# A searched order of one core's 2,098 operations, replaced by another searched order

## Chip, core and metric

The kernel runs on one core of a Trainium2 chip, in one launch. The core has five engines with a queue each: TensorE (PE; its weight loads are listed as PEld), VectorE (DVE), ScalarE (ACT), GpSimd (POOL) and SyncE (SP), which issues nearly all transfers here. An engine runs its own queue strictly in order and waits for others through semaphores. The metric is the time of one execution on the device in microseconds; smaller is better. The median of three runs is compared.

## What is computed

A linear-attention layer (a state of 48 x 48 per head, decayed by `w` at each step) over 4 batches, 8 heads and 768 steps, and behind it a feed-forward layer whose gate is a sigmoid of a short convolution:

```python
def _attn_ref(r, k, v, w, u):
    for t in range(S):
        cur = np.einsum('bhd,bhe->bhde', u[None] * kt, vt)
        y[:, :, t] = np.einsum('bhd,bhde->bhe', rt, state + cur)
        state = wt[:, :, :, None] * state + np.einsum('bhd,bhe->bhde', kt, vt)
...
def _moe_ref(x, w_in, conv_w, w_out):
    h = np.maximum(x @ w_in, 0.0)
    for k in range(K):
        conv_out += conv_w[k][None, None, :] * hp[:, k:k + S, :]
    gate = 1.0 / (1.0 + np.exp(-conv_out))
    return (h * gate @ w_out).astype(np.float32)
```

`x` is the attention's output with the heads side by side, 384 wide; `w_in` is 384 x 1024, `w_out` 1024 x 384, the convolution has three taps. `moe_w_in`, `moe_conv_w` and `moe_w_out` come as 64-bit floats and are turned into pairs of 32-bit numbers on the chip.

## The kernel before

The sequence is cut into 24 chunks of 128 steps, six for each batch. One chunk goes through these steps, named by their lines:

- Loads of `w`, `k`, `r`, `v` (L560, on SP). ScalarE rearranges a little of each (L583, operation `fill`). TensorE turns w, k and r (L605 for chunks 0 to 7; from chunk 8 on as half-transposes, L735, in two sets `f1` and `f2` around the scores of the chunk before). VectorE zeroes four columns of the bank that holds w (L575, `pad`), runs two scans over w (L615 and L623, a reciprocal L619 between them) and multiplies them into k and r (L620, L627).
- The rest of each head's rows is brought to a tile `last`: by TensorE (L636, `gather`) for chunks 0 to 3, by six small transfers (L644) for the others. TensorE turns the scaled keys back (L668 or within L735), ScalarE copies them (L677, L678).
- GpSimd multiplies r, k and u (L652, L654), VectorE sums (L655), GpSimd writes the sums on the diagonal of a tile `pm` (L658). TensorE makes the scores (L719), VectorE copies the upper triangle of them into `pm` (L751, twice a chunk).
- The state: TensorE L765, VectorE adds it to the decayed old one (L769, or L771 for a batch's first chunk), with ScalarE and GpSimd preparing the old one (L704, L707, L711). The output of the chunk: TensorE L781 (from the state) and L796 (within the chunk); ScalarE and VectorE write it as a high and a low part into `xT` (L800, L801).

A block of the feed-forward layer is 384 steps, half a batch: eight times a product with `w_in` (L810, three operations of three matmuls each), the gate (ScalarE L822, L823, L828, L831; VectorE L824, L826, L829; GpSimd L832), and then for three groups of 128 rows a product with `w_out` of eight operations (L839), an output copy (L867) and a store (L868). Weights are loaded in pieces of up to 1152 KB (L538, L546), and each 128 x 384 of them is converted by ScalarE (L490, L492), VectorE (L494, L497) and GpSimd (L499), and split (L478, L479). The small convolution weights are loaded by L523 and converted in four VectorE instructions (L463, L467, L469, L471), one of ScalarE (L465, which needs L463) and one of GpSimd (L473).

Nothing is scheduled by the compiler. The program records its 2,098 operations with their dependences (`Plan.op`) and then issues them in the order of a table, `ORDER`. A negative entry is a warm-up matmul of no use to the result (L446) into the bank of that number. Another table, `PLACES`, gives to each tile, in the order in which they are first needed, the slot of its store: 8 PSUM banks, 12 strips of 384 columns, 6 tiles for loaded w, k, r, 6 for weights and so on. So the tables set each engine's queue and which earlier use of a slot a new tile has to wait for.

```python
        for i in ORDER:
            if i < 0:
                self.warm(self.spare[-1 - i])
                continue
            _, _, f, deps, bufs = self.ops[i]
            assert deps <= done
            for b in bufs:
                if b.t is None:
                    b.t = b.view(b.store[next(places)])
            f()
```

Ahead of the table's operations stand a few fixed ones: five junk matmuls (L369), constants and zeroed tiles. Operation 20 broadcasts u with two matmuls (L650).

Of the kernel before, what the change touches and what calls it, by code (L numbers as in the profile page):

```python
# [28 lines left out]
    190, 0, 1, 2, 231, 51, 192, 20, 194, 4, -8, -8, -8, -8, -8, -8, -8, -8, -8, -8, -8, 198, -8, -8, -8, -8, 8, 191,  # L29
    60, 197, 200, 202, 205, 5, 6, 21, -8, -8, -8, -8, 11, -8, -8, -8, -8, 16, 22, 23, 238, 7, 10, 12, 13, 15, 17,  # L30
    52, 55, 24, 235, 53, 239, 210, 25, 56, 241, 243, 54, 246, 195, 196, 9, -4, -4, -4, -4, -4, -4, 18, 19, 199, 206,
    201, 207, 203, 182, 26, 183, -2, 208, 57, 211, 63, 212, 279, 68, 70, 71, 233, 237, 247, 248, 184, 62, 61, 64,
    214, 232, 272, 27, 14, 28, 236, 276, 209, 58, 251, 213, 252, 65, 216, 69, 59, 75, 215, 240, 280, 242, 3, 273,
    274, 278, 277, 431, 222, 185, 282, 284, 244, 224, 77, 186, 78, 253, 223, 287, 255, 72, 218, 292, 293, 249, 193,
    234, 29, 256, 435, 257, 76, 79, 439, 219, 181, 220, 217, 440, 221, 281, 250, 204, 288, 283, 225, 187, 227, 266,
    228, 289, 285, 432, 433, 275, 476, 82, 478, 477, 634, 296, 226, 294, 438, 290, 259, 441, 258, 260, 267, 443,
    446, 32, 188, 80, 262, 73, 254, 74, 286, 229, 81, 300, 295, 230, 30, 436, 297, 31, 291, 301, 455, 33, 437, 298,
    66, 44, 261, 456, 34, 189, 39, 46, -5, -5, 442, 263, 265, 264, 304, 37, 40, 306, 447, 268, 269, 38, 303, 302,
    299, 480, 484, 45, 270, 485, 35, 47, 305, 41, 67, 48, 98, 97, 309, 271, 448, 310, 311, 482, 444, 99, 457, 100,
    483, -3, -3, -3, 459, 83, 101, 500, 36, 312, 307, 486, 488, 491, 85, 86, 492, 92, 308, 493, 357, 358, 359, 346,  # L40
    347, 348, 481, 42, 84, 49, 90, 245, 91, 461, 102, 360, 361, 460, 638, 43, 87, 103, 487, 50, 463, 501, 362, 363,
    93, 94, 104, 349, 350, 489, 121, 107, 351, 352, 674, 453, 451, 747, 449, 434, 450, 454, 452, 120, 119, 364, 105,
# [900 lines left out]
```

## Time and profile before

| what | value |
|---|---|
| median of 3 runs | 335.58 us (334.97 to 335.73) |
| the profiled execution, and its span | 335.81 us, 333.5 us |
| TensorE busy, weight loads busy | 320.4 us (96%), 299.4 us (90%) |
| VectorE, ScalarE, GpSimd busy | 259.0 us (78%), 233.0 us (70%), 182.4 us (55%) |
| bytes moved, mean rate | 39.30 MB, 118 GB/s |
| granted TensorE clock, mean | 0.997 |

Busy time is the union of an engine's records. A matmul's record includes its way through the engine and overlaps the next one's, so that a stretch can be full of matmuls though one could start sooner; a weight load belongs to each matmul, and these do not overlap. The shares are means over the span: VectorE is full in the first third and half empty in the last. The span runs from the first to the last instruction; the rest of the execution's time lies around it.

### The profile page before, as it was taken

How to read it: one execution, taken by the hardware profiler on the slowest of the kernel's cores; microseconds unless marked ns; L12 is line 12 of the kernel's file. 1: busy time of each engine (PE TensorE's matmuls, PEld its weight loads, DVE VectorE, ACT ScalarE, POOL GpSimd, SP SyncE). 2: the span in 40 equal slices, each digit the busy share in tenths (PEclk: the TensorE clock that was granted, in tenths of full speed). 3: DMA queues.
4: the chain of work that ended last, by engine and by line, in shares of the span. 5: the costliest groups of instructions: out<-in, count | busy, mean ns of one | idle time of the engine just before them, and what ended most of it. 6: DMA issues, size and time to landing. Idle time of an engine off the chain costs nothing.

```text
span 333.5 us, 10276 instructions
## 1 busy us (share of the span) xinstructions
PE 320.4 (96%) x3979; PEld 299.4 (90%) x3979; DVE 259.0 (78%) x508; ACT 233.0 (70%) x644; POOL 182.4 (55%) x221
## 2 busy tenths in 40 slices
PE   8789999999999999999999999999999999999994
PEld 5668888898989899998999999999999999999994
DVE  1999999999998889988877988869876885575200
ACT  3369999998895478778776576846766768885411
POOL 7368997988874650378465440295525414533600
PEclk9999999999999999999999999999999999999998
DMA  7988969735254685466226836218400650000005
GB/s 144 242 178 220 247 170 232 248 73 109 42 113 79 138 235 139 107 176 128 56 61 131 234 88 135 63 33 173 108 3 17 200 168 0 2 0 2 0 22 197
DMA packets 113818, 39.30 MB, mean 118 GB/s; under 512 B 102349, under 2 KB 109286, under 8 KB 113766
## 3 DMA queue, kind: packets, MB, share of 16 engines
q1 hardware_dynamic: 113764, 38.61, 47.5%
q8 instruction: 32, 0.52, 0.7%
q14 instruction: 20, 0.16, 0.2%
q10 hardware_dynamic: 2, 0.00, 0.0%
HBM read 31.88 MB, written 4.72 MB: 110 GB/s over the span
## 4 chain that ended last, share of the span: by engine, by line
PE 49%; DMA 2%; DVE 1%; ACT 1%; issue 0%; SPq 0%; ACTq 0%
PE bank L839 22%; PE bank L810 16%; PE bank L719 3%; PE bank L796 3%; PE bank L735 2%; PE bank L781 2%; DMA nat<-in_w_dram 2%; PE bank L765 1%; DVE strip L824 1%; DVE strip L826 0%; ACT strip L823 0%; DVE strip L829 0%; DVE kr L620 0%; ACT strip L828 0%; ACT strip L867 0%
## 5 line engine op out<-in xcount | busy, mean ns | idle before, releaser
L810 PE MATMUL bank<-xT,wi 128*128 128x386 f32 x576 | 112.3, 343 | 1.3 <-DVE strip L497 0.7
L839 PE MATMUL bank<-wo,gh 128*128 128x384 f32 x576 | 109.2, 339 | 0.2 <-DVE strip L497 0.2
L810 PEld LDWEIGHTS bank<-xT,wi 128*128 128x128 f32 x576 | 100.9, 189 | 4.1 <-DVE strip L497 1.0
L839 PEld LDWEIGHTS bank<-wo,gh 128*128 128x128 f32 x576 | 100.5, 188 | 1.4 <-DVE strip L497 0.5
L832 POOL TENSOR_TENSOR gh<-strip,gh 128x384 fp32r<-128x384 f32 x64 | 64.5, 1025 | 58.9 <-ACT gh L831 48.2
L824 DVE SCALAR_TENSOR_TENSOR strip<-bank,cw,strip 128x384 f32<-128x384 f32 x64 | 38.2, 609 | 13.2 <-ACT strip L823 13.1
L829 DVE TENSOR_TENSOR strip<-bank,strip 128x384 f32<-128x384 f32 x64 | 34.7, 553 | 13.1 <-ACT strip L828 11.0
L828 ACT ACTIVATE strip<-strip 128x384 f32<-128x384 f32 x64 | 32.6, 522 | 14.1 <-DVE strip L826 14.0
L658 POOL TENSOR_SCALAR_AFFINE_SELECT pm<-dg 128x1024 f32<-128x1024 f32 x24 | 27.2, 1133 | 24.9 <-DVE dg L655 18.8
L822 ACT ACTIVATE bank<-bank 128x386 f32<-128x386 f32 x64 | 30.1, 478 | 14.5 <-PE bank L810 14.2
L826 DVE SCALAR_TENSOR_TENSOR strip<-bank,cw,strip 128x384 f32<-128x384 f32 x64 | 38.5, 613 | 1.2
L823 ACT ACTIVATE strip<-bank,cw 128x384 f32<-128x384 f32 x64 | 36.6, 580 | 3.1 <-DMA out_dram<-strip 1.0
L751 DVE COPY_PREDICATED pm<-upper,bank 128x512 f32<-128x512 int32 x48 | 33.9, 735 | 6.2 <-PE bank L719 4.5
L652 POOL TENSOR_TENSOR strip<-nat,nat 128x384 f32<-128x384 f32 x24 | 24.4, 1017 | 23.4 <-PE bank L796 8.6
L831 ACT CAST gh<-strip 128x384 fp32r<-128x384 f32 x64 | 31.6, 510 | 4.0 <-DVE strip L829 3.9
L796 PE MATMUL bank<-pm,strip 128*32 128x128 f32 x384 | 25.2, 273 | 0.0
L796 PE MATMUL bank<-pm,vz 128*32 128x128 f32 x384 | 24.9, 272 | 0.0
L654 POOL TENSOR_TENSOR strip<-strip,ubc 128x384 f32<-128x384 f32 x24 | 24.4, 1019 | 0.6
L867 ACT COPY strip<-bank 128x384 f32<-128x384 f32 x24 | 11.2, 477 | 18.5 <-PE bank L839 18.0
L615 DVE TENSOR_TENSOR_SCAN kr<-bank,one_end 128x387 f32<-128x387 f32 x24 | 22.8, 951 | 1.4 <-DMA last<-kr 0.5
L623 DVE TENSOR_TENSOR_SCAN kr<-bank,dA 128x387 f32<-128x387 f32 x24 | 22.9, 956 | 0.4
L583 ACT COPY nat<-nat 128x96 f32<-128x96 f32 x72 | 18.4, 269 | 7.0 <-DMA nat<-in_w_dram 3.9
(104 smaller groups left out, 518.3 us busy)
## 6 DMA issues: line engine op xcount, KB each, us to landing
gh<-in_moe_w_out_dram SPq DMA_DIRECT2D x5, 1152.0 KB, 6.9
nat<-in_w_dram SPq DMA_DIRECT2D x24, 192.0 KB, 3.6
nat<-in_k_dram SPq DMA_DIRECT2D x24, 192.0 KB, 3.6
nat<-in_r_dram SPq DMA_DIRECT2D x24, 192.0 KB, 3.7
gh<-in_moe_w_in_dram SPq DMA_DIRECT2D x4, 1152.0 KB, 7.3
strip<-in_v_dram SPq DMA_DIRECT2D x24, 192.0 KB, 3.2
out_dram<-strip SPq DMA_DIRECT2D x24, 192.0 KB, 2.1
last<-kr SPq DMA_DIRECT2D x120, 16.2 KB, 2.4
```

What stands on the lines that cost most here:

```text
L751: op("DVE", "cp", lambda g=g: nc.vector.copy_predicated(out=pm.t[:, g], mask=upper.unsqueeze(1).to_broadcast([P, NP, L]), data=sc[g].t.rea ...
L796: nc.tensor.matmul(rows(a, 32), lhsT=lhs, rhs=pm.t[:, g, j, :], start=(c == 0 and i == 0), stop=(i == 3), skip_group_check=True)
L810: nc.tensor.matmul(t.t[:, 0:xs.stop - xs.start], lhsT=wi[:, m, a, f * P:(f + 1) * P], rhs=xT[:, x0 + m, c, xs], start=(m == 0 and j == 0), ...
L822: ("ACT", "relu", lambda: nc.scalar.activation(out=h(0, width + 2), in_=h(0, width + 2), func=AF.Relu), [t], [t]),
L823: ("ACT", "mul", lambda: nc.scalar.mul(out=a(), in_=h(1), mul=cw[:, 1, fs]), [t, "cw"], [a1]),
L824: ("DVE", "stt", lambda: nc.vector.scalar_tensor_tensor(out=a(), in0=h(0), scalar=cw[:, 0, fs], in1=a(), op0=ALU.mult, op1=ALU.add), [t], ...
L826: ("DVE", "stt", lambda: nc.vector.scalar_tensor_tensor(out=a(), in0=h(2), scalar=cw[:, 2, fs], in1=a(), op0=ALU.mult, op1=ALU.add), [t], ...
L828: ("ACT", "sig", lambda: nc.scalar.activation(out=a(), in_=a(), func=AF.Sigmoid), [], [a1]),
L829: ("DVE", "gate", lambda: nc.vector.tensor_tensor(out=g.t[:, 0:width], in0=h(1), in1=a(), op=ALU.mult), [t, a1], [g]),
L831: ("ACT", "cast", lambda: nc.scalar.copy(out=part(0)[:, 0:width], in_=g.t[:, 0:width]), [g], [key]),
L832: ("POOL", "lo", lambda: nc.gpsimd.tensor_tensor(out=part(1)[:, 0:width], in0=g.t[:, 0:width], in1=part(0)[:, 0:width].bitcast(F32), op=AL ...
L839: nc.tensor.matmul(acc.t[:, 0:DM], lhsT=part(a)[:, tt * P:(tt + 1) * P], rhs=wo[:, f, c, :], start=(f == 0 and a + c == 0), stop=(f == FT ...
```

## The change

The tables `ORDER` and `PLACES` are replaced; the rest of the file is the same. The same 2,098 operations are issued in another order, with 29 warm-up matmuls in place of 35. The new order was searched for with some slack added to each hand-over between engines and to each transfer, and with longer steps on all engines but TensorE.

```diff
 ORDER = [
-    190, 0, 1, 2, 231, 51, 192, 20, 194, 4, -8, -8, -8, -8, -8, -8, -8, -8, -8, -8, -8, 198, -8, -8, -8, -8, 8, 191,
...
+    0, 1, 190, 51, 4, 20, -8, 8, 2, 231, 191, 192, 3, 55, 7, 52, 10, 56, 197, 194, 53, 5, 12, 54, 238, -8, -8, -8,
...
```

Three places show what moves. In the rows, a number behind a tile's name tells its slot, so that `kr_139` and `kr_140` are two of three slots for scaled keys, and `strip_119` in L463 to L471 is the loaded convolution weights.

The first is the head of VectorE's queue behind its fixed instructions. Before:

```order
L575 MEMSET bank_65 128x4
L615 SCALAR_TENSOR_TENSOR kr_139<-bank_65,one_end 128x387
L619 RECIPROCAL dA_137<-kr_139 128x3
L623 SCALAR_TENSOR_TENSOR kr_139<-bank_65,dA_137 128x387
L575 MEMSET bank_69 128x4
L575 MEMSET bank_66 128x4
L615 SCALAR_TENSOR_TENSOR kr_140<-bank_66,one_end 128x387
L619 RECIPROCAL dA_137<-kr_140 128x3
L620 TENSOR_TENSOR kr_140<-bank_67,kr_140 128x3x128
L623 SCALAR_TENSOR_TENSOR kr_140<-bank_66,dA_137 128x387
L627 TENSOR_TENSOR kr_140<-bank_68,kr_140 128x3x128
L463 TENSOR_SCALAR bank_70<-strip_119 24x128
```

And now:

```order
L469 TENSOR_SCALAR bank_66<-strip_119 24x128
L575 MEMSET bank_65 128x4
L463 TENSOR_SCALAR bank_67<-strip_119 24x128
L615 SCALAR_TENSOR_TENSOR kr_139<-bank_65,one_end 128x387
L471 SCALAR_TENSOR_TENSOR strip_121<-strip_119,bank_66 24x128
L575 MEMSET bank_66 128x4
L619 RECIPROCAL dA_137<-kr_139 128x3
L467 SCALAR_TENSOR_TENSOR strip_122<-strip_119,bank_67 24x128
L575 MEMSET bank_68 128x4
L623 SCALAR_TENSOR_TENSOR kr_139<-bank_65,dA_137 128x387
L615 SCALAR_TENSOR_TENSOR kr_140<-bank_66,one_end 128x387
L620 TENSOR_TENSOR kr_139<-bank_69,kr_139 128x3x128
```

Two of the four instructions on the convolution weights and one bank's zeroing now stand ahead of the first scan, and the first scans are those of chunk 0, where they were those of chunk 1.

The second is the head of SP's queue, all loads. Before:

```order
L560 DMA nat_131<-in_w_dram 128x8x48
L560 DMA nat_132<-in_w_dram 128x8x48
L560 DMA nat_133<-in_k_dram 128x8x48
L560 DMA nat_134<-in_r_dram 128x8x48
L560 DMA nat_135<-in_w_dram 128x8x48
L523 DMA strip_119<-in_moe_conv_w_dram 24x256
L560 DMA nat_136<-in_r_dram 128x8x48
L560 DMA nat_131<-in_k_dram 128x8x48
L538 DMA gh<-in_moe_w_in_dram 128x3x768
L560 DMA nat_132<-in_r_dram 128x8x48
L560 DMA nat_133<-in_k_dram 128x8x48
L560 DMA nat_134<-in_w_dram 128x8x48
```

And now:

```order
L560 DMA nat_134<-in_r_dram 128x8x48
L560 DMA nat_135<-in_w_dram 128x8x48
L560 DMA nat_136<-in_k_dram 128x8x48
L560 DMA nat_131<-in_r_dram 128x8x48
L560 DMA strip_120<-in_v_dram 128x8x48
L538 DMA gh<-in_moe_w_in_dram 128x3x768
L560 DMA nat_133<-in_r_dram 128x8x48
L560 DMA nat_132<-in_k_dram 128x8x48
L560 DMA nat_134<-in_w_dram 128x8x48
L560 DMA nat_135<-in_r_dram 128x8x48
L538 DMA gh<-in_moe_w_in_dram 128x3x768
L560 DMA strip_128<-in_v_dram 128x8x48
```

The four rows ahead of these, not shown, are the loads of w and k of chunk 0, w of chunk 1 and the convolution weights, which stood sixth. The second piece of `w_in` stands fifteenth now and ahead of a `v` (of chunk 1), where it stood nineteenth and behind three of them.

The third is VectorE's queue around the zeroing of the bank for the transposed w of chunk 12, on which the half-transposes of TensorE behind it wait (the last row of each piece). Before:

```order
L824 SCALAR_TENSOR_TENSOR strip_122<-bank_64,cw,strip_122 128x384
L826 SCALAR_TENSOR_TENSOR strip_122<-bank_64,cw,strip_122 128x384
L751 COPY_PREDICATED pm_159<-upper,bank_65 128x512
L615 SCALAR_TENSOR_TENSOR kr_140<-bank_66,one_end 128x387
L619 RECIPROCAL dA_137<-kr_140 128x3
L623 SCALAR_TENSOR_TENSOR kr_140<-bank_66,dA_137 128x387
L751 COPY_PREDICATED pm_159<-upper,bank_70 128x512
L620 TENSOR_TENSOR kr_140<-bank_69,kr_140 128x3x128
L627 TENSOR_TENSOR kr_140<-bank_71,kr_140 128x3x128
L829 TENSOR_TENSOR strip_119<-bank_64,strip_122 128x384
L575 MEMSET bank_66 128x4
```

And now:

```order
L615 SCALAR_TENSOR_TENSOR kr_140<-bank_68,one_end 128x387
L655 TENSOR_REDUCE dg_157<-strip_129 128x4x2
L769 TENSOR_TENSOR sd_167<-bank_65,sd_166 112x192
L619 RECIPROCAL dA_137<-kr_140 128x3
L623 SCALAR_TENSOR_TENSOR kr_140<-bank_68,dA_137 128x387
L620 TENSOR_TENSOR kr_140<-bank_71,kr_140 128x3x128
L627 TENSOR_TENSOR kr_140<-bank_70,kr_140 128x3x128
L751 COPY_PREDICATED pm_159<-upper,bank_66 128x512
L655 TENSOR_REDUCE dg_158<-strip_119 128x4x2
L751 COPY_PREDICATED pm_159<-upper,bank_69 128x512
L575 MEMSET bank_64 128x4
```

In both orders the same instructions stand ahead of that zeroing, in another sequence, but for the one L769, which stands right behind it in the old order.

## Rows read from the trace of the kernel before

**Rows 1.** Stretches: busy us (instructions) of each engine, granted clock, DMA.
```profile
core 0: us, PE busy (x) PEld busy (x) DVE busy (x) ACT busy (x) POOL busy (x), PEclk, DMA share, GB/s
8.00:20.00 12.00, 9.21 (x79) 7.47 (x77) 11.38 (x26) 4.88 (x18) 6.05 (x7) 1.00 0.91 215
20.00:40.00 20.00, 18.96 (x435) 16.63 (x439) 19.72 (x41) 17.94 (x60) 17.30 (x20) 1.00 0.89 210
40.00:60.00 20.00, 19.10 (x241) 16.81 (x231) 19.38 (x41) 18.90 (x53) 17.62 (x22) 1.00 0.74 200
60.00:80.00 20.00, 19.11 (x145) 17.81 (x137) 18.92 (x37) 18.14 (x46) 16.96 (x18) 1.00 0.52 150
80.00:108.00 28.00, 27.32 (x406) 25.20 (x406) 26.97 (x53) 22.26 (x69) 20.87 (x23) 1.00 0.44 87
```

**Rows 2.** Waits of VectorE: us in total, times, longest.
```profile
DVE bank L575 <- PE bank L605: 5.6, 1, 5.6
```

**Rows 3.** Timeline of VectorE, 7 to 14 us: start, us, instruction, idle before.
```profile
7.61 0.06 DVE L575 MEMSET bank<- 128x4 f32 x1 [5.61 <-PE bank L605]
7.78 0.96 DVE L615 TENSOR_TENSOR_SCAN kr<-bank,one_end 128x387 f32<-128x387 f32 x1
...
13.43 0.27 DVE L463 TENSOR_SCALAR bank<-strip 24x128 int32<-24x128 int32 x1
```

**Rows 4.** Timeline of ScalarE, 3 to 8 us, and of SP, 4 to 6.
```profile
3.64 0.27 ACT L583 COPY nat<-nat 128x96 f32<-128x96 f32 x1 [0.79 <-DMA nat<-in_w_dram]
...
5.57 0.27 ACT L583 COPY nat<-nat 128x96 f32<-128x96 f32 x1 [0.68 <-DMA nat<-in_k_dram]
...
4.75 0.98 SPq L523 DMA_DIRECT2D strip<-in_moe_conv_w_dram  x1
```

**Rows 5.** Timeline of TensorE, 4 to 8.2 us.
```profile
4.47 2.53 PE L446 MATMUL bank<-ident 128*128 128x256 bf16 x11
6.79 0.74 PE L605 MATMUL bank<-ident,nat 128*128 128x128 f32 x3
...
7.80 0.49 PE L605 MATMUL bank<-ident,nat 128*128 128x128 f32 x3
```

**Rows 6.** VectorE by line, 8 to 108 us: busy us, mean ns, idle before.
```profile
L826 DVE SCALAR_TENSOR_TENSOR strip<-bank,cw,strip 128x384 f32<-128x384 f32 x16 | 9.7, 614 | 0.4
L824 DVE SCALAR_TENSOR_TENSOR strip<-bank,cw,strip 128x384 f32<-128x384 f32 x16 | 9.5, 607 | 0.0
...
L829 DVE TENSOR_TENSOR strip<-bank,strip 128x384 f32<-128x384 f32 x16 | 8.5, 549 | 0.3
...
L655 DVE TENSOR_REDUCE dg<-strip 128x8 f32<-128x384 f32 x10 | 5.4, 539 | 0.0
```

**Rows 7.** Timeline of VectorE and of TensorE at 108 us.
```profile
108.32 0.36 DVE L769 TENSOR_TENSOR sd<-bank,sd 112x192 f32<-112x192 f32 x1 [0.76 <-PE bank L735]
108.33 0.06 DVE L575 MEMSET bank<- 128x4 f32 x1
...
108.90 0.53 PE L735 MATMUL bank<-ident,nat 64*128 64x64 f32 x9
```

**Rows 8.** Waits of TensorE's weight loads, 108 to 329 us.
```profile
PEld bank L735 <- ACT sbd L711: 1.0, 1, 1.0
PEld bank L735 <- DVE xT L801: 0.9, 1, 0.9
PEld bank L735 <- DVE strip L829: 0.8, 3, 0.3
```

**Rows 9.** Timeline of SP; DMA issues of the page (count, KB, us to landing).
```profile
21.25 1.03 SPq L538 DMA_DIRECT2D gh<-in_moe_w_in_dram  x1
...
gh<-in_moe_w_in_dram SPq DMA_DIRECT2D x4, 1152.0 KB, 7.3
```

**Rows 10.** TensorE by line: the warm-up matmuls in 0 to 6.7, then 6 to 13 us.
```profile
L446 PE MATMUL bank<-ident 128*128 128x256 bf16 x11 | 2.5, 418 | 0.0
...
L446 PE MATMUL bank<-ident 128*128 128x256 bf16 x23 | 3.9, 305 | 1.4 <-DVE kr L620 1.4
```

260 rows, old and new, of tables (ORDER, PLACES) are left out of this document.

## Prediction

> **What bounds the kernel now.** I read the stretches first, then the waits, then the two ends of the stretch that they point to. By its matmuls TensorE looks like the bound (27.32 of 28 us busy from 80 to 108 [rows 1]), but a matmul's record overlaps the next one's. The weight loads (PEld) do not overlap, and by them TensorE has 83.9 us of work in the 100 us from 8 to 108 (7.47 + 16.63 + 16.81 + 17.81 + 25.20) [rows 1]. In the same 100 us VectorE is busy for 96.4 us (11.38 + 19.72 + 19.38 + 18.92 + 26.97) [rows 1]. Its longest idle time is before that stretch: 5.6 us until its first memset, which waits for the first transposes [rows 2]; for 8 to 108 the view of its waits lists none at all. So the run has three parts: VectorE waits for its first input (to 7.6 us), VectorE sets the pace (to about 108 us), and then TensorE sets it. Only what VectorE has to do before a given TensorE step, and when it may start, moves the first two parts. In the third only waits of TensorE itself can be won.
>
> **Part 1, the start of VectorE.** Before, its queue begins with the memset and the scan of a chunk's turned w, at 7.61 and 7.78 us [rows 3]. The loads were there long before: ScalarE's small copies (L583) start as their loads land, the first at 3.64 us, the third at 5.57 [rows 4], one load about each 0.96 us ((5.57 - 3.64) / 2). What kept the scan was TensorE's own queue: the broadcast of u, then from 4.47 eleven warm-up matmuls, and only at 6.79 the first three transposes [rows 5]. In the new order one warm-up matmul stands between the broadcast and the first transposes, those of chunk 0. So these start at about 4.7 (4.47 and one warm-up at the eleven's spacing, (6.79 - 4.47) / 11 = 0.21) and are done at about 5.4 (0.74 us, as before) [rows 5]. VectorE's new first instruction is not the memset but the first word test of the conv weights (L469). Their load is issued fourth and not sixth, so two loads earlier: it was issued at 4.75 [rows 4], and two loads earlier in landing means about 5.7 us, just behind the third load's 5.57. Then L469, the memset and L463 go, 0.27 us each at most [rows 3], and the scan of chunk 0 starts at about 6.2 where the first scan started at 7.78. That is 1.6 us, and two of the four conv instructions are done besides (0.4 us), which before lay at 13.43 and behind [rows 3]. Against it stand small waits that the new queue may have in its first microseconds, for the transposes behind seven more warm-up matmuls: 0.62 us of idle lay in 8 to 20 before (12.00 - 11.38) [rows 1], and I let the new one have 0.4 more. Term: **-1.6 us**. Bounds: -2.0 if nothing waits; -0.4 if the conv load lands no earlier than the fifth load does now (about 7.5, 3.64 + 4 x 0.96), since then only the conv work is out of the way.
>
> **Part 2, what VectorE must have done.** Two points where TensorE has the same number of products, scores and chunks behind it in both orders can be compared. The first is the start of the output product for the second 128 rows of block 1 (L839, 24 such operations are done by then): VectorE's part ahead of it is the same list in both orders, but for one L824, one L826 and one L829 more and two L655 less. At 607, 614, 549 and 539 ns that is 0.607 + 0.614 + 0.549 - 2 x 0.539 = +0.69 us [rows 6]. The second is the memset of chunk 12's bank at 108.33 [rows 7], which the second half-transposes of that chunk wait for (L735 at 108.90 [rows 7]): ahead of it the same list stands in both, 195 instructions, plus one L769 in the new order, 0.36 us [rows 7], which the old one has just behind it. I take the mean, **+0.5 us** (0.3 to 0.7). In between the new order asks for more: the transposes of chunk 4's r stand behind 58 instructions of VectorE instead of 53, some 2.2 us more, and this is made up by the first of the two points. As long as VectorE stays as dense as it was, this moves TensorE's waits and not their sum. The new order has one more set of half-transposes (0.53 us [rows 7]) behind it at the second point: **-0.5 us** of TensorE work less after it.
>
> **Part 3, behind 108 us.** The products, scores and their operands are the same instructions. The view of TensorE's weight-load waits lists seventeen rows there, of 0.2 to 1.1 us, three of them in [rows 8]; most of the others are switches between kinds of matmul that any order has. If the three long ones for other engines went (1.0 for the state copy L711, 0.9 for L801, 0.8 for L829), 2.7 us would go; if the new order brings as many again, +2.7. No view says which. Two of the three are hand-overs at which VectorE was late (0.9 and 0.8), and it comes out of the second part earlier by its lead, so I let a third of these 1.7 us go, **-0.5 us**. Six warm-up matmuls fewer (29 for 35) cost and save nothing: they stand in waits of TensorE in the first 40 us, where VectorE sets the pace. The tail stays: both orders end in the same products and output copies.
>
> **Sum.** -1.6 + 0.5 - 0.5 - 0.5 = -2.1 us. The profiled execution took 335.81 us (333.5 of it the span), so 333.7 on its scale; it lies 0.23 us over the median of 335.58, so **333.5 us** for the median, from which the rivals are reckoned too. The ends of the terms give -2.0 + 0.3 - 0.5 - 2.7 = -4.9 (330.7) and -0.4 + 0.7 - 0.5 + 2.7 = +2.5 (338.1).
>
> **Rivals.**
> (a) *The conv load stops the start.* VectorE's and ScalarE's queues are in order, and the new orders put L469 first on the one and the conv exponent (L465) third on the other, ahead of the copies for k and r of chunk 0. If the load lands at 7.5, those copies wait for L463 and the lead shrinks to 0.4: -0.4 + 0.5 - 0.5 - 0.5 = -0.9, 334.7; with as much again lost to the late copies, 335.2. Against it: it has 24 KB where a load has 192, and goes out as the fourth.
> (b) *Slower: v of chunk 1 behind the second weight load.* Before, the second piece of w_in (1152 KB) went out at 21.25 [rows 9], behind v of chunks 1 and 2. In the new order that piece stands ahead of v of chunk 1, k of chunk 3 and v of chunk 2. Such a piece takes 7.3 us from issue to landing [rows 9]. If it is issued at 14 (the SP queue first has to get four loads past the first piece), v lands at about 22, and TensorE wants it for the state of chunk 1 at about 24: nothing is lost. If SP gets there only at 18, v lands at 26, VectorE's sum of the state (L769) waits two microseconds with all its queue behind it, and that is the whole lead. It decides the sign from an idle time of VectorE of about 2.8 us more between 8 and 108 (the 2.1 won and 0.67); with 4 us more the run takes 335.6 - 2.1 + 4 = 337.5.
> (c) *More is won behind 108*: all three long waits go, -2.1 - 2.2 = -4.3, 331.3.
> (d) *The clock stays low at the start.* The granted clock is 1.00 of 2.4 GHz in every stretch of [rows 1], yet the warm-up matmuls before 6.7 us take 418 ns and those behind 305 [rows 10], so TensorE ran at its lower level until then, and it had run junk and warm-up matmuls almost without a break. The new order has one warm-up matmul before its first set of transposes, seven before the second and five more up to the first gather, where the old one had eleven, four and fourteen. Should the lower level last until the first gather, five sets of transposes cost 0.25 us more each (0.74 against 0.49 [rows 5]), 1.25 us in which VectorE's lead is mostly gone: 333.5 + 1.25 = 334.8, and with later ones 335.4. The Trainium skill speaks for this rival: in TensorE: Matmul & The Clock Gate, Part 4: PE-mode transpose, it says that transposes do not count as busy for the clock the way matmuls do. The trace before doesn't show it either way, since warm-up matmuls and transposes alternate when the clock rises.
>
> **How the numbers follow.** The forecast has 0.45, (c) 0.17, both faster by over 0.2% (0.67 us, about what a measurement of this kernel can tell from no change: below 334.9). (a) has 0.12 and (d) 0.05, both within 0.2%. (b), and any like wait of VectorE in its dense stretch, has 0.21 and is slower. So faster 0.62, same 0.17, slower 0.21. The range goes from (c) and the lower end of the sum's bounds, 330.7, to just short of (b)'s 337.5, which leaves out a little under 2 in 10: 330.7 to 337.2.
>
> **What would show it.** Right: VectorE's first scan at 6 to 6.5 us; its busy time in the next 100 us still 96 or more; the memset of the bank that stood at 108.33 at about 107; the difference to before, about 1.5 us there, no smaller at 200. Wrong: a first VectorE instruction behind 7 us (a), a row of VectorE waiting on TensorE's L765 or L605 between 20 and 60 us (b), L446 or L605 at the longer duration behind 8 us (d). If VectorE keeps its lead to 108 us and the time is still 335.6 or more, Part 3 was mis-sized: the third part would then have its own waits that the first hid.

## The result, and the profile after

The new order takes 331.47 us (median of four runs, 330.77 to 331.76) against 335.27 for the old one beside it (334.75 to 335.73): the ratio is 0.9884, 95% interval 0.986 to 0.9908. That is 3.8 us faster, where 2.1 were forecast. The direction was right, the size was not, and the steps below show that most of the gain came by a way that the sum did not have. The profiled execution took 331.74 us, its span is 329.6.

The stretches of the new order, in the columns of [rows 1] (us, busy time of each engine, granted clock, share of DMA, GB/s):

```profile
8.00:20.00 12.00, 11.94 (x150) 10.46 (x149) 11.52 (x24) 7.68 (x28) 7.22 (x8) 1.00 0.95 248
20.00:40.00 20.00, 18.84 (x384) 16.23 (x383) 19.80 (x43) 18.48 (x61) 18.16 (x22) 1.00 0.88 222
40.00:60.00 20.00, 19.99 (x252) 18.36 (x251) 19.62 (x40) 18.47 (x52) 17.42 (x21) 1.00 0.81 204
60.00:80.00 20.00, 19.89 (x117) 19.50 (x116) 19.67 (x40) 19.94 (x51) 20.00 (x21) 1.00 0.56 141
80.00:108.00 28.00, 26.98 (x505) 24.39 (x507) 24.68 (x50) 19.23 (x62) 18.45 (x21) 1.00 0.65 147
```

VectorE is busy for 95.3 us of these 100 and was for 96.4, hardly a sign of 4 us won. The weight loads of TensorE rose from 83.9 to 88.9 us: it gets through more of its work in the same time. The start of VectorE (timeline: start, us, instruction, idle before), which answers to [rows 3]:

```profile
5.66 0.29 DVE L469 TENSOR_SCALAR bank<-strip 24x128 int32<-24x128 int32 x1 [3.67 <-DMA strip<-in_moe_conv_w_dram]
5.88 0.27 DVE L463 TENSOR_SCALAR bank<-strip 24x128 int32<-24x128 int32 x1
5.90 0.06 DVE L575 MEMSET bank<- 128x4 f32 x1
6.08 0.96 DVE L615 TENSOR_TENSOR_SCAN kr<-bank,one_end 128x387 f32<-128x387 f32 x1
```

This is as forecast: the conv weights land at 5.66, the first scan starts at 6.08 (forecast 6 to 6.5, before 7.78).

How far ahead the new order is can be followed along TensorE's own work. I gave each of its operations its usual time (the same in both orders, none for warm-up matmuls) and compared when the same sum is reached. The numbers are us against the old order's profile; minus is earlier:

| TensorE work done, us | new order | a_late | a_joined | a_swapped | b_early |
|---|---|---|---|---|---|
| 20 | -1.89 | -0.55 | -1.44 | -2.69 | -1.47 |
| 40 | -2.34 | -1.51 | -1.07 | -2.32 | -1.59 |
| 60 | -4.17 | -3.69 | -1.42 | -2.55 | -1.59 |
| 85 | -5.54 | -5.06 | -2.25 | -2.94 | -1.92 |
| 90 | -4.05 | -4.59 | -1.14 | -1.90 | -1.89 |
| 150 | -4.49 | -4.21 | -1.33 | -2.20 | -1.59 |
| 298 (all) | -4.95 | -5.08 | -2.08 | -3.21 | (see below) |

Three things stand in the first column. The lead grows all through VectorE's dense part, to 5.5 us, where about 1.5 were forecast. It falls by 1.5 us between 85 and 90, and 0.9 is won behind. And TensorE is done 4.95 us earlier, while the span is only 3.8 shorter: about 1.1 us more is spent behind the last matmul. Each had to be explained. Two more profiles of the same code (after_repeat, after_2) are 5.3 and 3.3 us ahead of the old order at 110 us of work, where this one is 4.35: two profiles of one code can lie 2 us apart, so a difference of less than that between two single profiles settles nothing by its size alone.

### The profile page after: what moved, and what is told of

Its sections match the earlier page's. It is cut to its first block, busy times and chain, and to the rows that moved or that the text cites. A ratio compares the mean times of both kernels' runs of the same rounds, so it can differ in the third digit from the quotient of the medians.

```text
span 329.6 us, 10262 instructions
## 1 busy us (share of the span) xinstructions
PE 320.0 (97%) x3973; PEld 299.4 (91%) x3973; DVE 257.3 (78%) x508; ACT 233.4 (71%) x644; POOL 182.8 (55%) x221
## 4 chain that ended last, share of the span: by engine, by line
PE 66%; DVE 12%; ACT 7%; DMA 5%; POOL 4%; issue 3%; SPq 2%; DVEq 0%; ACTq 0%; POOLq 0%
PE bank L839 25%; PE bank L810 24%; PE bank L719 4%; PE bank L796 4%; PE bank L735 3%; PE bank L781 3%; DMA strip<-in_v_dram 2%; DVE pm L751 2%; DMA nat<-in_w_dram 2%; DVE kr L623 1%; SPq L644 1%; DVE kr L615 1%; POOL wi L479 1%; PE bank L765 1%; DVE strip L497 1%
## 5 line engine op out<-in xcount | busy, mean ns | idle before, releaser
L832 POOL TENSOR_TENSOR gh<-strip,gh 128x384 fp32r<-128x384 f32 x64 | 65.5, 1044 | 56.2 <-ACT gh L831 44.9
L658 POOL TENSOR_SCALAR_AFFINE_SELECT pm<-dg 128x1024 f32<-128x1024 f32 x24 | 26.2, 1096 | 21.4 <-DVE dg L655 19.7
L583 ACT COPY nat<-nat 128x96 f32<-128x96 f32 x72 | 19.2, 270 | 12.9 <-DMA nat<-in_w_dram 5.8
L796 PE MATMUL bank<-pm,strip 128*32 128x128 f32 x384 | 26.0, 274 | 0.1
L796 PE MATMUL bank<-pm,vz 128*32 128x128 f32 x384 | 25.3, 273 | 0.0
L615 DVE TENSOR_TENSOR_SCAN kr<-bank,one_end 128x387 f32<-128x387 f32 x24 | 22.9, 955 | 1.4 <-PE bank L735 0.5
L623 DVE TENSOR_TENSOR_SCAN kr<-bank,dA 128x387 f32<-128x387 f32 x24 | 22.9, 953 | 0.2
```

Source lines behind the costliest of these rows:

```text
L796: nc.tensor.matmul(rows(a, 32), lhsT=lhs, rhs=pm.t[:, g, j, :], start=(c == 0 and i == 0), stop=(i == 3), skip_group_check=True)
L832: ("POOL", "lo", lambda: nc.gpsimd.tensor_tensor(out=part(1)[:, 0:width], in0=g.t[:, 0:width], in1=part(0)[:, 0:width].bitcast(F32), op=AL ...
```

## Experiments

### Where VectorE's time went: pairs put back, pairs taken apart

VectorE's instructions may be looked at one by one: where does each start, measured from the end of the one before? In the old order, up to the scores (L719) that start at 100.41 us, there are two main kinds. An instruction that reads what the one right before it wrote starts 0.07 us behind that one's end. One whose operands have long been there starts 0.09 us *before* that end. Fifteen others lie between, and none waits more than 0.15 us. Here is the first kind in the trace of the old order (start, us), a scan and its two followers:

```profile
40.62 0.94 DVE L615 TENSOR_TENSOR_SCAN kr<-bank,one_end 128x387 f32<-128x387 f32 x1
41.60 0.18 DVE L619 RECIPROCAL dA<-kr 128x3 f32<-128x3 f32 x1
41.81 0.96 DVE L623 TENSOR_TENSOR_SCAN kr<-bank,dA 128x387 f32<-128x387 f32 x1
42.69 0.41 DVE L494 TENSOR_SCALAR bank<-gh 128x256 int32<-128x256 int32 x1
```

40.62 + 0.94 is 41.56 and L619 starts at 41.60, L623 at 41.81 where L619 ended at 41.78; but L494, which needs none of them, starts at 42.69 where L623 ends at 42.77. The new order puts other work between. The same steps of the next chunk:

```profile
36.44 0.95 DVE L615 TENSOR_TENSOR_SCAN kr<-bank,one_end 128x387 f32<-128x387 f32 x1
37.31 0.40 DVE L497 CUSTOM_DVE_ANT_0 strip<-bank,strip 128x512 uint16<-128x512 uint16 x1
37.62 0.17 DVE L619 RECIPROCAL dA<-kr 128x3 f32<-128x3 f32 x1
37.71 0.53 DVE L801 TENSOR_TENSOR xT<-bank,xT 128x384 fp32r<-128x384 f32 x1
38.15 0.95 DVE L623 TENSOR_TENSOR_SCAN kr<-bank,dA 128x387 f32<-128x387 f32 x1
39.02 0.53 DVE L801 TENSOR_TENSOR xT<-bank,xT 128x384 fp32r<-128x384 f32 x1
39.47 0.34 DVE L769 TENSOR_TENSOR sd<-bank,sd 112x192 f32<-112x192 f32 x1
```

Every start lies 0.08 or 0.09 us ahead of the end before it. The kernel **a_joined** undoes this alone: 23 pairs are put back to back. Its edit at the place just shown:

```diff
 L615 SCALAR_TENSOR_TENSOR kr_141<-bank_69,one_end 128x387
+L619 RECIPROCAL dA_137<-kr_141 128x3
+L623 SCALAR_TENSOR_TENSOR kr_141<-bank_69,dA_137 128x387
 L497 ISA strip_128<-bank_66,strip_128 128x512
-L619 RECIPROCAL dA_137<-kr_141 128x3
 L801 TENSOR_TENSOR xT<-bank_65,xT 128x3x128
-L623 SCALAR_TENSOR_TENSOR kr_141<-bank_69,dA_137 128x387
 L801 TENSOR_TENSOR xT<-bank_67,xT 128x3x128
```

> The new order with 23 pairs of VectorE's instructions put back to back again, between 12 and 90 us, each pair a producer and the instruction that reads its result, as the old order had them (one or two other instructions are moved out from between); nothing else is moved. Theory H (hand-overs): in the old order's trace a VectorE instruction that reads what the one right before it wrote starts 0.07 us behind that one's end (38 pairs, mean 0.068), and one whose operands lie ready starts 0.07 us before it (136 pairs, mean -0.074), so each pair put back costs 0.14 us while VectorE sets the pace: 23 x 0.14 = 3.2 us, so 331.5 + 3.2 = 334.7, or 333.5 if a third of them fall where TensorE sets the pace. Theory S (start and work ahead of TensorE alone, as forecast): the same instructions in nearly the same places, 331.5, at most 0.4 more.

Measured: 335.75 us, ratio to the old order 1.0005 (0.999 to 1.002). **The whole gain is gone.** On the same chip a_late, which has the new order's VectorE queue, took 331.5. In a_joined's trace the same seven instructions take:

```profile
36.45 0.94 DVE L615 TENSOR_TENSOR_SCAN kr<-bank,one_end 128x387 f32<-128x387 f32 x1
37.43 0.18 DVE L619 RECIPROCAL dA<-kr 128x3 f32<-128x3 f32 x1
37.64 0.96 DVE L623 TENSOR_TENSOR_SCAN kr<-bank,dA 128x387 f32<-128x387 f32 x1
38.52 0.40 DVE L497 CUSTOM_DVE_ANT_0 strip<-bank,strip 128x512 uint16<-128x512 uint16 x1
38.84 1.01 DVE L801 TENSOR_TENSOR xT<-bank,xT 128x384 fp32r<-128x384 f32 x2
39.77 0.35 DVE L769 TENSOR_TENSOR sd<-bank,sd 112x192 f32<-112x192 f32 x1
```

From the start of L615 to that of L769 it is 3.32 us and was 3.03: 0.29 for two pairs, 0.145 each. In the progress table a_joined is 3.3 us behind the new order at 85 us of work (0.45 at 20), and 23 x 0.14 is 3.2. Its runs, against those of a_late, lost about one microsecond more than its profile (334.58, the fastest of twelve); that rest is not explained.

The objection is that exchanges as such might cost, wherever they stand. **a_swapped** moves one of the same two instructions at 22 of the places, by one place, but makes no new pair. At the first two of them:

```diff
+L771 COPY sd_165<-bank_67 112x192
 L497 ISA strip_126<-bank_69,strip_126 128x768
-L771 COPY sd_165<-bank_67 112x192
...
-L619 RECIPROCAL dA_137<-kr_139 128x3
 L655 TENSOR_REDUCE dg_157<-strip_127 128x4x2
+L619 RECIPROCAL dA_137<-kr_139 128x3
```

> Control for a_joined: the new order with 22 exchanges of two neighbouring VectorE instructions at the same 22 places, each moving one of the same two instructions by one place, but so that no further pair stands back to back (51 such pairs in the whole program, as in the new order; a_joined had 76). Theory H: what costs is the instruction right behind the one whose result it reads, not the moving: 331.5, at most 0.6 more. Rival M (any exchange in a dense order costs, since other engines wait for what comes later): 333 to 335, as in a_joined.

Measured: 333.06 us, ratio 0.9939 (0.9916 to 0.9962), about 2 us above the new order (after_repeat, on the same chip, took 331.19) and, by the ratios, 2 below a_joined. So theory H missed here: exchanges do cost. In time this control does not part the two causes. Behind TensorE's last matmul a_swapped needs 4.22 us where the new order needs 5.34 (see The end), which may hide 1.1 us of its loss, and at all of TensorE's work it is 1.7 us behind the new order, a_joined 2.9, with single profiles. What parts them is how the time went, and the trace shows that. The four longest waits of VectorE in a_swapped (us in total, times, longest), 8 to 98 us:

```profile
DVE kr L627 <- issue: 1.2, 1, 1.2
DVE pm L751 <- ACT junk L612: 0.8, 1, 0.8
DVE strip L829 <- ACT strip L828: 0.6, 1, 0.6
DVE sd L771 <- PE bank L765: 0.4, 1, 0.4
```

For the first the view names no releaser; TensorE's transposes (L605) end at 61.44 us, and L627 starts at 61.49. The new order has, from 8 to 96 us, these alone:

```profile
DVE kr L627 <- PE bank L605: 0.4, 1, 0.4
DVE pm L751 <- ACT junk L612: 0.3, 1, 0.3
DVE bank L494 <- DMA gh<-in_moe_w_out_dram: 0.3, 1, 0.3
```

All hand-overs of VectorE up to the same scores, sorted by kind. In the columns stand the count and the sum of the times from one instruction's end to the next one's start; a minus is overlap. "Dependent" reads what the one right before it wrote; a wait is a gap over 0.15 us:

| kernel | first instr. | work of all instr. | dependent | overlapping | other, up to 0.15 | waits | scores start |
|---|---|---|---|---|---|---|---|
| old order | 7.61 | 99.71 | 40, +2.72 | 125, -10.84 | 15, +0.51 | 0 | 100.41 |
| new order | 5.66 | 100.00 | 5, +0.24 | 152, -13.00 | 21, +0.92 | 3, +1.06 | 95.82 |
| a_joined | 5.82 | 100.33 | 27, +1.50 | 132, -11.29 | 17, +0.61 | 5, +1.13 | 99.03 |
| a_swapped | 5.54 | 100.19 | 5, +0.24 | 151, -12.92 | 18, +0.81 | 7, +3.78 | 98.42 |
| b_apart | 7.72 | 100.64 | 11, +0.68 | 149, -12.88 | 16, +0.77 | 6, +2.95 | 100.74 |
| b_early | 5.59 | 99.79 | 40, +2.71 | 124, -10.75 | 15, +0.51 | 1, +0.24 | 98.80 |
| a_late | 5.56 | 99.87 | 5, +0.24 | 155, -13.20 | 19, +0.67 | 2, +2.22 | 96.30 |

a_joined and the new order differ by 3.21 us: +1.26 of dependent hand-overs and +1.71 of lost overlap, and their waits are alike (1.13 and 1.06). a_swapped and the new order differ by 2.60, and 2.72 of it are waits. So a dependent pair has a price of its own, and an order that takes pairs apart must also bring no wait. This is the new order's doing: 35 pairs fewer, and one microsecond of waits for it. The sums hold beyond the single profiles. Sorted by the sign of the gap alone, up to the same scores, the gaps above zero and up to 0.15 us sum to 3.2 us in each of three profiles of the old order's VectorE queue (before, b_tail9, b_tail9_2) and to 0.9 to 1.1 in three of the new order's (after, after_repeat, after_2); the overlap is 12.6 to 12.8 and 15.1 to 15.7 us. What differs between executions of the new order is its waits, 0.8 to 2.0 us.

**b_apart** tries the converse: the old order with 26 pairs taken apart. At its place for the reciprocal:

```diff
 L615 SCALAR_TENSOR_TENSOR kr_140<-bank_68,one_end 128x387
-L619 RECIPROCAL dA_137<-kr_140 128x3
 L620 TENSOR_TENSOR kr_141<-bank_64,kr_141 128x3x128
+L619 RECIPROCAL dA_137<-kr_140 128x3
```

> The old order with 26 such pairs of VectorE taken apart, between 12 and 98 us, by exchanging one of the two with a neighbour whose operands are long there; the start, the loads and all other engines keep their order. Theory H: 26 x 0.14 = 3.6 us less while VectorE sets the pace, so 331.7 if all of it reaches the end and 333.0 if a third is lost again in TensorE's own waits. Theory S: no gain, 335.3, or up to 0.5 more since some results come half a microsecond later.

Measured: 334.12 us, ratio 0.996 (0.9933 to 0.9986): 1.6 us won of the 2.3 to 3.6 expected. Its profile is one of its three slowest executions of twelve (335.89), so it tells little about the size, but it shows what eats the gain: hand-overs are 4.1 us better (-2.04 of dependent ones, -2.04 of overlap), waits 2.95 worse, and the instructions themselves take 0.93 longer. Exchanging neighbours by hand trades most of one for the other. The longest of these waits of VectorE is for TensorE's transposes (L605, 1.2 us), and TensorE's weight loads in turn lost 1.6 us at 52 us on the copy of a load that landed at 54.04. I took that load for the cause, and **b_apart_load** issues it earlier:

```diff
 L560 DMA nat_132<-in_w_dram 128x8x48
+L560 DMA nat_133<-in_k_dram 128x8x48
 L644 DMA last_145<-kr_139 16x2x130 x2
...
 L546 DMA gh<-in_moe_w_out_dram 128x3x768
-L560 DMA nat_133<-in_k_dram 128x8x48
```

> As b_apart (the old order with 26 dependent pairs of VectorE taken apart), and the load of chunk 6's k is issued four places after the first piece of w_out instead of behind its second piece, since its place is free from 37.4 us on. Theory HT (hand-overs, then a transfer): in b_apart TensorE was 1.14 us ahead of the old order by 35 us of work and lost 1.5 us waiting for the copy of that load, which landed at 54.04 and was used at 54.07; in the old order itself it lands at 53.55 and is used at 53.58, so it holds the old order too. With the load at 46 or so this wait goes and the gain of the pairs behind it stays: 334.1 - 1.5 = 332.6, and TensorE 1 to 2.5 us ahead of the old order from 40 to 100 us of its work. Rival (pairs taken apart only trade one wait for another, of ScalarE's or TensorE's results): 333.8 to 334.3 again.

Measured: 335.14 us, ratio 0.9983 (0.9959 to 1.0006). That theory fell. In the trace the wait of TensorE's weight loads at this place is 0.7 us instead of 1.6, but 1.4 us, where b_apart lost 0.5, are lost at 30 us, ahead of a gather (L636) for which the profile names no releaser, and nothing is won in the time.

### The start

**b_early** gives the old order the early start alone, and **a_late** takes it from the new one. The edit of b_early takes ten warm-up matmuls, each with its weights, from ahead of the first transposes and puts them behind the second set; the two rows stand ten times:

```diff
 L446 MATMUL bank_71<-ident 128x256
-L446 LDWEIGHTS ident
-L446 MATMUL bank_71<-ident 128x256
```

The edit of a_late adds ten ahead of the new order's first transposes:

```diff
 L650 MATMUL bank_64<-ubc,ones_f 128x384
+L446 LDWEIGHTS ident
+L446 MATMUL bank_71<-ident 128x256
```

> The old order with ten of its eleven first warm-up matmuls moved from ahead of the first transposes to behind the second set; nothing else is changed. VectorE's first scan then starts at about 6 us and not 7.78. If the start's lead passes in full, as forecast, 335.3 - 1.6 = 333.7; by theory H the rest of the measured 3.8 us is not here, so no lower than 333.3. If VectorE only waits later for the next transposes or for loads, 335.0 to 335.3.

> The new order with ten more warm-up matmuls (eleven for one) ahead of the first transposes, as the old order had them; nothing else is changed. VectorE's first scan then starts at about 8.1 us and not 6.08. If the lead of the start passes to the end in full, 331.5 + 2.0 = 333.5. If TensorE or the loads absorb it (the start was not what counted), 331.5 to 332.0.

Measured for b_early: 334.91 us, ratio 0.9976 (0.9951 to 1.0001). In its profile the first scan starts at 5.76, and the lead of 1.6 us passes unchanged through VectorE's whole dense part to 150 us of work (the last column of the progress table); between 150 and 200 this execution, the slowest of twelve, loses 3 us, and the granted clock is 0.97 in the stretch from 200 to 260. So the start is worth 1.6 in a trace and 0.85 in the median, with an interval that just reaches none.

Measured for a_late: 331.5 us, ratio 0.9877 (0.9853 to 0.9901), **the same as the new order**. The trace shows that the start did slip:

```profile
5.56 0.28 DVE L469 TENSOR_SCALAR bank<-strip 24x128 int32<-24x128 int32 x1 [3.56 <-DMA strip<-in_moe_conv_w_dram]
7.69 0.27 DVE L463 TENSOR_SCALAR bank<-strip 24x128 int32<-24x128 int32 x1 [1.85 <-issue]
7.72 0.06 DVE L575 MEMSET bank<- 128x4 f32 x1
7.89 0.96 DVE L615 TENSOR_TENSOR_SCAN kr<-bank,one_end 128x387 f32<-128x387 f32 x1
```

Behind it, a_late is 1.3 us later than the new order at 20 us of TensorE's work, 0.5 at 85, and not at all at the end, by one profile each. Behind 8 us VectorE has one wait of 0.3 us where the new order has 1.06 us in three, and TensorE's weight loads wait 0.5 us for the state copies of ScalarE (L711) where the new order's wait 1.5, nearly all of it in one place, told below. In this pair of profiles, what VectorE wins at the start the new order gives back in waits for other engines. The two times say the same, but their intervals are 0.8 us to either side, and a_tail (below), which starts as early as the new order, has a single wait of 0.33 us up to the scores in its profile; so the start is worth at most about a microsecond here, and not surely nothing.

Last, **b_apart_load_early** has b_apart's pairs, the load and the start together; its last edit is that of b_early.

> As b_apart_load, and ten of the first eleven warm-up matmuls are moved behind the second set of transposes, as in b_early. If hand-overs, this transfer and the start are the three things that the new order changed, and add up: 332.6 - 1.6 = 331.0, about the new order's 331.5. If the start is worth nothing once VectorE is dense (as in a_late, where it made no difference to the new order), 332.3 to 332.8.

Measured: 332.99 us, ratio 0.993 (0.9905 to 0.9955), near the second of the two expected: 2.1 us below b_apart_load in the median, and 2.6 below the old order, where the new one is 4.1 below it. In the old order's family the start counts, and my own exchanges reach two thirds of what the new order has.

### Where the lead falls at 106 us

The timeline of the new order's ScalarE, and behind it TensorE's one long wait there, from the view of its waits:

```profile
105.58 0.27 ACT L583 COPY nat<-nat 128x96 f32<-128x96 f32 x1 [4.52 <-DMA nat<-in_r_dram]
105.76 0.33 ACT L707 ACTIVATE sd<-sd,last 112x48 f32<-112x48 f32 x1
106.18 0.72 ACT L711 COPY sbd<-sd 48x192 f32<-48x192 f32 x2
```

```profile
PE bank L781 <- ACT sbd L711: 1.0, 1, 1.0
```

A copy that is wanted later (L583, the last chunk's r) stands in ScalarE's queue ahead of the state copies and waits 4.5 us for its load; with it wait L707 and L711, and TensorE. **a_best** has ScalarE's copy behind them, and the change of a_tail, told below:

```diff
-L583 COPY nat_131<-nat_131 128x2x3x16
 L707 ACTIVATE sd_168<-sd_167,last_146 112x48
 L711 COPY sbd_150<-sd_168 48x4x48 x2
+L583 COPY nat_131<-nat_131 128x2x3x16
```

> As a_tail, and ScalarE's copy of the last chunk's r (L583) stands behind the three instructions for the state (L707, L711, L711) and not ahead of them. In the new order's trace that copy waits 4.5 us for its load (landed 105.56), the state copies behind it start at 105.76, and TensorE waits 1.02 us for them at 106.58. Then that wait goes, 0.5 to 1.0 us of it reaching the end: 330.4 - 0.8 = 329.6. If VectorE or a transfer stands right behind it, 330.4 again.

Measured: 330.13 us, ratio 0.9841 (0.9819 to 0.9863), against a_tail's 329.82 on the same chip. The wait (at 105.21 us in a_tail) is gone, and another stands three microseconds behind it, at 108.50; TensorE's waits in that stretch are now

```profile
PE bank L839 <- POOL gh L832: 0.6, 1, 0.6
```

In the profile TensorE ends 0.44 us earlier than in a_tail; the medians show nothing. **a_best2** is a_best with one more pair taken apart:

```diff
+L824 SCALAR_TENSOR_TENSOR strip_125<-bank_64,cw,strip_125 128x384
 L497 ISA strip_129<-bank_67,strip_129 128x768
-L824 SCALAR_TENSOR_TENSOR strip_125<-bank_64,cw,strip_125 128x384
```

> The new order with the end as in a_tail, ScalarE's copy of the last chunk's r behind the state copies as in a_best, and one more dependent pair of VectorE (L494, L497 at 70 us) taken apart. By theory H and C: no late ScalarE at the end (-1.1), TensorE's 1.02 us wait at 106 us gone (-0.4 in a_best's profile against a_tail's), the pair 0.14: 331.5 - 1.1 - 0.4 - 0.1 = 329.9. If the wait at 106 us only gives way to another, as a_best's median suggests (330.13 against a_tail's 329.82), 330.3.

Measured: 329.77 us, ratio 0.9839 (0.9803 to 0.9875), beside 331.19 for the new order (after_repeat, ratio 0.9877, 0.9845 to 0.9908). It is the lowest median here, 1.4 us below the new order's, but the two intervals overlap, and the run does not tell how much of that is the copy, the pair or the change of a_tail.

> The new order itself once more, on the same chip as the next three. A second profile of the same code shows how far one execution's progress may differ from another's (a_tail, with the same order, was up to 1.3 us ahead of the new order's first profile at 85 us of TensorE's work, and 1.7 us faster where its end alone should have given 1.1). If a_tail's surplus of 0.6 us is such a difference between executions and chips: 330.8 to 331.5 and a progress that differs from the first profile's by up to 1 us. If it is not: 331.5 and the progress within 0.3 us of the first profile's.

Its profile is 0.95 us ahead of the new order's first one at 110 us of work, so the first of the two cases came.

### The end

Behind TensorE's last matmul the old order needs 4.22 us to the end of the span, the new one 5.34. The waits of SP in the last 11 us name it:

```profile
SPq L938 <- ACTq L911: 1.2, 1, 1.2
SPq L938 <- PEq L938: 0.6, 2, 0.5
```

L911 is the branch around the general code. ScalarE goes on 0.46 us behind it in the old order (330.17 to 330.63), 3.72 in the new one (325.04 to 328.76), and the last barrier waits for it. ScalarE runs the same 757 instructions ahead of the branch in both; the skipped code's first part has nine of ScalarE's instructions in the new order and eight in the old. **b_tail9** gives the old order a ninth, in code that never runs:

```diff
-        q.dma_start(out=uT, in_=u.rearrange("(m g) d -> (g d) m", g=2))
+        [q.dma_start(out=uT[:, h:h + 2], in_=u.rearrange("(m g) d -> (g d) m", g=2)[:, h:h + 2]) for h in (0, 2)]
```

> The old order with the load of u in the general branch, which is jumped over, issued in two halves: ScalarE has one instruction more there, nine for eight as in the new order, and nothing that runs is changed. Theory C (place of ScalarE's code behind the jump): ScalarE goes on 3.6 us or more behind its branch and not 0.46, and the end comes 1.1 us later, 335.6 + 1.1 = 336.7. Rival (the new order's late ScalarE comes from something else in it): 0.46 us again, 335.6.

In its trace ScalarE goes on 3.44 us behind the branch, and the end comes 5.25 us behind the last matmul. The median was 335.33 against 335.26, ratio 1.0007 (0.9988 to 1.0027). **a_tail** takes seven of these instructions from the new order, by the same load from another queue:

```diff
-        q.dma_start(out=uT, in_=u.rearrange("(m g) d -> (g d) m", g=2))
+        nc.gpsimd.dma_start(out=uT, in_=u.rearrange("(m g) d -> (g d) m", g=2))
```

> The new order with one line changed in the general branch, which these inputs do not take: its load of u is issued by GpSimd and not by ScalarE, so that ScalarE has seven instructions fewer to jump over at the end (2 and not 9 in the branch's first block; the old order has 8). Theory C (code of ScalarE behind the jump): in the old order's trace ScalarE goes on 0.46 us after its branch, in the new order's 3.72 us after it, and SP waits 1.16 us for that at the very end, in all three profiles of the new order's family and in none of the old's. If it is the place of the code behind the jump, the wait goes and the time is 331.5 - 1.1 = 330.4. Rival (it comes from the order of the last copies and stores): 331.5, ScalarE again 3.6 us or more behind its branch.

Measured: 329.82 us, ratio 0.9824 (0.98 to 0.9848), and ScalarE goes on 0.45 us behind the branch. But the end is not shorter: 5.22 us behind the last matmul, since now VectorE's last drain is late, and SP waits for the final round of the barrier instead:

```profile
SPq L938 <- PEq L938: 1.6, 2, 1.4
SPq L911 <- SPq L911: 0.5, 1, 0.5
```

Since the one median had not risen and the other had fallen for no reason in the trace, I ran the three once more on one chip.

> The new order once more, beside a_tail_2 and b_tail9_2 on one chip. 331.2 to 331.5 by its earlier medians; ScalarE late behind its last branch (3.6 to 4.0 us) as in each profile of it.

> a_tail once more, on the same chip as after_2. Theory C (the late ScalarE at the end costs about 1.1 us in every execution): 1.1 us below after_2, 330.1 to 330.4. Rival (it is late in the profiled execution only, and a_tail's lower median came from another chip): the same as after_2 within 0.4.

> b_tail9 once more. Theory C: 1.0 us above the old order's median on this chip. Rival (late in the profiled execution only): the old order's median within 0.4, as in the first runs of it (335.33 against 335.26), though its trace had ScalarE 3.44 us behind its branch and the span 5.25 us behind TensorE's last matmul for 4.22.

Measured: after_2 331.94 us (ratio 0.9869, 0.9833 to 0.9905), a_tail_2 330.89 (0.9871, 0.9842 to 0.9901), b_tail9_2 336.63 against 335.6 (1.0026, 1.0009 to 1.0044). The ratios of the first two do not differ. The number of ScalarE's instructions up to the code behind the jump decides whether it is late, not the skipped part by itself: a_swapped has nine there like the new order, but one fewer ahead of the branch (756 for 757; its trace has 791 records of ScalarE's queue for 792), and it goes on 0.46 us behind the branch, with an end of 4.22 us. With 757 + 8 = 765 or fewer each profile is in time, with 766 each is late, and b_tail9 changes nothing else. That the lateness costs a microsecond of time is shown once of twice on the old order's side; why a_tail's medians are lower, with an end as long as the new order's, stays open.

## Why the prediction was right and wrong

- **What bounds the kernel.** Right that VectorE sets the pace to about 108 us (in the new order to 103). The step that failed is what I took from it: busy 96.4 us of 100 and no wait in the view, so nothing to win but the start. A busy share counts an engine as full whether its instructions overlap by 0.09 us or stand 0.07 apart. At 180 hand-overs this came to 4.2 us, and no row of the wait view names a gap that small. The timeline would have told it: consecutive rows, the end of one against the start of the next. One reading ahead of the prediction is wrong without harm: narrow weight loads do overlap (from 249.96 us five rows of L796, of 0.11 to 0.20 us, start within 0.13), but 83.9 us is the time in which any of them ran.
- **Part 1, the start.** Right in its place: first scan at 6.08, conv load at 5.66, so rival (a) is out. The term of -1.6 holds in the old order (b_early's trace). In the new order no more than a microsecond of it is left, and none in the medians (a_late). The forecast's largest term is thus not what made the new order faster.
- **Part 2, the work ahead.** At a third point, the scores, VectorE's work ahead is 100.00 us for 99.71, +0.3 (forecast 0.3 to 0.7 at its two points). But "as long as VectorE stays as dense as it was" was a condition, and it did not hold: dependent hand-overs gave -2.48, overlap -2.16, other small gaps +0.41, together -4.23, against +1.06 of waits. The memset of chunk 12's bank, forecast at about 107, came at 102.78 (before 108.33 [rows 7]).
- **Part 3, behind.** From that point to the last matmul the lead went from 5.54 to 4.95, so +0.6 where -0.5 was forecast, within the bounds of 2.7: one new wait of TensorE (1.0 us, by ScalarE's queue), and something won behind.
- **The tail.** "The tail stays" was wrong by 1.1 us in the profile.
- **The sum** in the two profiles: -1.95 (VectorE's first instruction) - 4.23 + 1.06 + 0.53 (longer instructions, and TensorE's answer to the last of them) = -4.59 at the scores, -0.95 from there to the half-transposes of chunk 12 (TensorE's weight loads wait 0.2 us for 0.6, VectorE for them 0.2 for 0.8), then +0.59 and +1.12 (end): -3.83 of the span.
- **The rivals.** (b) did not come: the weight piece went out at 15.52, and no row of VectorE waiting for the state is there. (c) named a time of 331.3, close to the result, for a wrong reason: on balance nothing was won behind 108. (d) came in its sign, at a smaller price, as told next.

The prediction's sign of (d) was L446 or L605 at the longer duration behind 8 us. In the new order these warm-up matmuls and transposes take 421 ns each up to 9.82 us and 273 from 10.20 on; in the old one 421 up to 7.01 and 273 from 7.37 (the granted clock of the stretches is given as 1.00 throughout, so the durations alone tell it). Three rows of the new order, each six transposes, at the long duration, at both, and at the short one:

```profile
7.45 1.51 PE L605 MATMUL bank<-ident,nat 128*128 128x128 f32 x6 [0.44 <-issue]
9.39 1.19 PE L605 MATMUL bank<-ident,nat 128*128 128x128 f32 x6
12.31 0.82 PE L605 MATMUL bank<-ident,nat 128*128 128x128 f32 x6
```

VectorE has one wait for L605 there, 0.44 us at 10.28, and not the 1.25 of the rival. a_late does not test (d), since its long durations last to 10.14 us too. The order alone does not set the moment: the old order and a_late run the same kinds of matmuls up to 7.2 us, and in six profiles that share the new order's VectorE queue and start, the short durations begin at 7.98 (a_best), 9.22 (a_tail), 9.76 (a_tail_2), 10.20 (the new order), 11.63 (after_repeat) and 13.38 us (after_2). VectorE's waits from 6 to 20 us are 0, 0, 0.22, 0.44, 0.44 and 1.31 us in these, so part of the difference between executions arises here. What decides the moment, no run shows.

The Trainium skill bears on the pairs at two places. Perfetto Trace Analysis, Per-engine timelines, says that VectorE's reported time ends with the acknowledgement of its writes, while the next instruction may begin to read when the first has left the engine's arithmetic: the trace agrees, with starts 0.09 us ahead of the reported end where nothing is waited for. VectorE: DVE Perf Modes, The DRAIN you can't avoid, says that a semaphore after each of eight copies cost nothing extra. Here the trace differs: an instruction that has to see the one before it complete comes 0.145 us later than one that has not, and the 23 pairs of a_joined cost 3.3 us of progress.

## What to carry to other kernels

On the engine that sets the pace, read consecutive rows of the timeline, not its busy share: here an instruction that reads its immediate predecessor's result cost 0.14 us more than an independent one, and the run with 23 such pairs put back lost the whole gain of 4 us, 3.3 of it in the trace. Put an instruction whose operands are ready between the two, and look at once whether some other engine now gets its input late: of the 3.6 us that the 26 exchanges made by hand were to win, 1.6 came, and the trace shows waits in place of most of the rest. A lead at the start is worth something only if the rest of the order does not give it back; whether it does is seen by taking the lead away from the faster version, not by adding it to the slower.

## What the runs showed of the hardware

One more instruction of ScalarE in code that is never run moved its continuation behind the branch from 0.46 to 3.44 us, with the same instructions executed; one fewer ahead of the branch, in a_swapped, moved it back to 0.46. In both orders' traces five transfers of code (8 and 16 KB) start in the last 3.4 us, so I take it that the code behind the jump had to be fetched; which engine each of them served, the trace does not say, and no run shows it. With seven instructions fewer ScalarE was in time and VectorE late. TensorE's first warm-up matmuls and transposes took 421 ns each, and 273 later, and the moment of the change differs between executions: the last long ones started at 9.82, 10.91 and 13.01 us in three executions of the new order. And two executions of one code may be 2 us apart along VectorE's dense part (5.3 and 3.3 us ahead of the old order at 110 us of work), so a single profile does not settle less than that.
